# One reduction for the maxima of 16 scores, another layout of the scores, another buffer for the blocks' diagonal

## The chip, the cores and the metric

The kernel runs on one core of a Trainium2 chip. The core has a matrix engine (TensorE, PE in the profile), a vector engine (VectorE, DVE), a scalar engine (ScalarE, ACT), GpSimd (POOL) and SyncE (SP), whose queue here issues all transfers. Each takes its own instructions in the order in which they were written, and waits on semaphores for the others. The metric is the time on the device of one execution, in microseconds; several runs are made and the median is given.

## The reference

Two layers are computed, each made of the same two sublayers on 2048 tokens of 512 values. The first is a Fourier mixing, the second a product-key mixture of experts:

```python
def _A_ref(x, dft_seq_re, dft_seq_im, dft_hid_re, dft_hid_im):
    a = jnp.einsum("bsd,ed->bse", x, dft_hid_re)
    b = jnp.einsum("bsd,ed->bse", x, dft_hid_im)
    y = jnp.einsum("ts,bse->bte", dft_seq_re, a) - jnp.einsum("ts,bse->bte", dft_seq_im, b)
    return y

def _B_ref(x, w_q, k1, k2, u, v):
    ...
    s1 = jnp.einsum("nhd,ed->nhe", q1, k1)
    s2 = jnp.einsum("nhd,ed->nhe", q2, k2)
    i1 = jnp.argsort(-s1, axis=-1)[..., :K]
    i2 = jnp.argsort(-s2, axis=-1)[..., :K]
    t1 = jnp.take_along_axis(s1, i1, axis=-1)
    t2 = jnp.take_along_axis(s2, i2, axis=-1)
    cand = (t1[..., :, None] + t2[..., None, :]).reshape(BS, H, K * K)
    eidx = (i1[..., :, None] * E + i2[..., None, :]).reshape(BS, H, K * K)
    ord2 = jnp.argsort(-cand, axis=-1)[..., :K]
    top_s = jnp.take_along_axis(cand, ord2, axis=-1)
    top_e = jnp.take_along_axis(eidx, ord2, axis=-1)
    g = _softmax(top_s, axis=-1)
    ue = u[top_e]
    ve = v[top_e]
    act = _gelu(jnp.einsum("nd,nhkd->nhk", xf, ue))
    out = jnp.einsum("nhk,nhk,nhkd->nd", g, act, ve)

x = x + _A_ref(_layernorm(x, axis=-1), ...)
x = x + _B_ref(_layernorm(x, axis=-1), ...)
```

H is 32 heads, E 16 values in each of two halves (the two key sets), K is 2. So for every token, head and half the two largest of 16 scores are wanted with their places; of the four pairs the two best experts; and the 256 experts' activations are weighted by what all heads chose.

## The kernel before, in words

**Stages.** The hidden DFT is applied after the one along the sequence. `seq_unit` (line 434) multiplies the normalised tokens by a 256-token wide block of the sequence matrices (L518): 16 steps of 128 tokens, four accumulators, three matmuls for each, since all 32-bit numbers are split in a high and a low part. The blocks come from memory, and ACT and DVE split them (L458, L462). The result goes to `pth` and `ptl` (L543, L546). Seven units are 256 tokens wide; the last 256 tokens are two units of 128. `token_tile` (line 566) does everything else for 128 tokens: the hidden DFT (L615), the sum into the row (L625), the layer norm (L245 to L271), its transpose (L664 to L674), the scores (L694, L698) and the experts' inner products (L725), the search of the two largest, the weights, the output (L1044, L1048) and the sum into the row (L1064). There are 32 token tiles, 16 in each layer.

**Order.** Nothing is scheduled by hand. Each step is an `Op` with an engine, a duration by formula (`dve` at line 153, `act` at 157; a hop between dependent instructions of 0.13 us for DVE, line 76), what it follows, which buffers it takes and gives back, and a priority. `Plan.run` (line 89) plays the list through with these durations and draws the order on every engine from it. A pool in `BUFS` (line 176) gives the number of buffers; a `Hold` is one buffer taken from the first to the last user. PE's steps of token tiles get `late` 1.0 us in most of the program (line 121): the planner counts their inputs as so much later. The priority `FINAL` is that of the very last token tile, called `fine` in the code. Where PE has a gap behind the last sequence step, matmuls whose result nobody reads are put in (L1137).

**The search.** `f_sc` (L700) has ACT copy the scores of a half from PSUM (there as head, value) into `t["sc"]`, kept as value, half, head. `chain` (L773) then works on 16 x 64 scores. `tree32` (L781) takes the largest by four maxima of pairs, of 8, 4, 2 and 1 times 64 values; the partial results lie in `tmp`, the last goes to `val`. `eq` (L776) compares all scores with it, `codes` (L815) turns hits into place numbers, `tree16` (L795) reduces them to the place, `f_one` and `f_off` (L825, L829) push the found score far down, and the same is done again for the second. `flat` and `four` (L752, L755) are views of the scores and of `eq`. For the last token tile (`HALVED`) the two halves are separate chains of half the width. The small instructions from L854 to L892 choose the pairs and their weights; `q` is transposed (L903) and copied to `qt` (L907).

**The masks and the blocks.** For each half `hf` of the heads' groups, two masks `t["m", hf, r]` are made from `qt` (L926), the second is multiplied by the weights (L932), and PE multiplies them (L943). They take one `"lr"` buffer each, of four. The blocks' diagonal is copied by ACT (`f_gs`, L955) to `t["gs"]`, which takes a buffer of the pool `"sc"`, the one in which the scores lie; that pool has one buffer. From there SP sends it to memory and back in another order (L999, L1006), and DVE multiplies the activations by it (`f_weigh`, L1014). In the last token tile of a wide unit before the end (`spare_p`), and in the last of all, `gs` lies in the place of `pth` instead; the last token tile uses other buffers for its masks too, and no memory.

Of the kernel before, what the change touches and what calls it, by code (L numbers as in the profile page):

```python
# [8 lines left out]
F32 = mybir.dt.float32  # L9
# [7 lines left out]
P = 128  # L17
# [10 lines left out]
H = 32  # L28
# [124 lines left out]
def dve(n, rate=1):  # L153
    return 0.069 + n / (0.96e3 * rate)
# [11 lines left out]
def spectral_peer_kernel(ctx: ExitStack, tc, x_in, cseq, ctile, dhid, wq, k1t, k2t, ut, vm, out):  # L166
# [7 lines left out]


    BUFS = {"acc": 4, "bank": 4, "raw": 4, "c": 3, "p": 1, "row": 4, "wr": 5, "wp": 2,
            "tok": 3, "sc": 1, "eq": 1, "act": 3, "q": 2, "top": 1, "qt": 1, "lr": 4, "gt": 1, "pp": 1, "gdr": 2, "bn": 1}
    plan = Plan(BUFS)


# [47 lines left out]
    def work(shape, dtype, name, pool=None):  # L228
        return work_pool().tile(shape, dtype, name=name, bufs=BUFS[pool or name])
# [336 lines left out]
    def token_tile(layer, n, i, t0, at):  # L566
# [119 lines left out]
        for hf in range(2):  # L686
            hb = Hold("bank")

            def f_pch(hf=hf, ks=ks[0]):
                if ks.start == 0:  # L690
                    t["pc", hf] = bank([P, H, E])
                for k in range(ks.start, ks.stop):
                    for r in (wh, wl):
                        nc.tensor.matmul(t["pc", hf], t["th"][:, k, :], r[:, k, hf], start=(k == 0 and r is wh), stop=False)  # L694

            def f_pcl(hf=hf):
                for k in range(KD):
                    nc.tensor.matmul(t["pc", hf], t["tl"][:, k, :], wh[:, k, hf], start=False, stop=(k == KD - 1))  # L698

            def f_sc(hf=hf):  # L700
                if hf == 0:
                    t["sc"] = work([P, E, 2, H], F32, "sc")
                nc.scalar.copy(t["sc"][:, :, hf, :], t["pc", hf].rearrange("p h e -> p e h"))  # L703
# [12 lines left out]
            sc_parts.append(op("ACT", act(512), f_sc, [a_pe] + sc_parts, take=[hsc] if hf == 0 else [], last=[hb], prio=prio))  # L716
# [35 lines left out]
        def four(name):  # L752
            return t[name].rearrange("p e (f h) -> p e f h", f=2)

        def flat(name):  # L755
            return t[name].rearrange("p e f h -> p e (f h)")


        halved = HALVED(layer, at)
# [5 lines left out]
        def new():  # L765
            if "val" not in t:
                t["val"] = work([P, 2, 64], F32, "val", "top")
                t["tmp"] = work([P, E // 2, 64], F32, "tmp", "eq")
                t["eq"] = work([P, E, 64], F16, "eq")
                t["q"] = work([P, 3, 2, 2, H], F16, "q")  # L770
                t["key"] = work([P, 2, H], F16, "key", "top")

        def chain(z, fs, cols, w, after, prio):  # L773
            nf = fs.stop - fs.start

            def eq(rank_):  # L776
                def f():
                    nc.vector.tensor_tensor(t["eq"][:, :, cols], flat("sc")[:, :, cols], val(rank_, cols), op=ALU.is_equal)  # L778
                return f

            def tree32(rank_, after):  # L781
                def f0():
                    new()
                    nc.vector.tensor_max(t["tmp"][:, :, cols], flat("sc")[:, :8, cols], flat("sc")[:, 8:, cols])  # L784

                a = [op("DVE", dve(8 * w), f0, after, take=[heq, hq, htop] if rank_ == 0 and z == 0 else [], prio=prio)]
                for m in (4, 2, 1):
                    def f(m=m):
                        s = t["tmp"][:, :, cols]
                        o = s[:, :m] if m > 1 else t["val"][:, rank_, cols][:, None, :]  # L790
                        nc.vector.tensor_max(o, s[:, :m], s[:, m:2 * m])
                    a = [op("DVE", dve(w * m), f, a, prio=prio)]
                return a

            def tree16(dst, after):  # L795
                a = after
                for m in (8, 4, 2):
                    def f(m=m):
                        s = t["eq"][:, :, cols]
                        nc.vector.tensor_max(s[:, :m], s[:, :m], s[:, m:2 * m])  # L800
                    a = [op("DVE", dve(w * m, 2), f, a, prio=prio)]

                def f():
                    x, y = (t["eq"][:, m, cols].rearrange("p (f h) -> p f h", h=H) for m in (0, 1))
                    dst(x, y)
                return [op("DVE", 0.12, f, a, prio=prio)]

            def key1(x, y):
                x, y = (m[:, :, None, :].to_broadcast([P, nf, 2, H]) for m in (x, y))
                nc.vector.tensor_max(t["q"][:, fs, 0], x, y)  # L810

            def key2(x, y):
                nc.vector.tensor_max(t["key"][:, fs], x, y)

            def codes(after):  # L815
                def f():
                    e = four("eq")[:, :, fs]
# [3 lines left out]
            a = tree32(0, after)  # L821
            a = codes([op("DVE", dve(16 * w), eq(0), a, prio=prio)])
            a = tree16(key1, a)

            def f_one():  # L825
                k = t["q"][:, fs, 0, 0, :][:, None, :, :].to_broadcast([P, E, nf, H])
                nc.vector.tensor_tensor(four("eq")[:, :, fs], io[:, :, fs], k, op=ALU.is_equal)

            def f_off():  # L829
                s = flat("sc")[:, :, cols]  # L830
                nc.vector.scalar_tensor_tensor(s, t["eq"][:, :, cols], -BIG, s, op0=ALU.mult, op1=ALU.add)

            a = op("DVE", dve(16 * w, 2), f_one, a, prio=prio)
            a = op("DVE", dve(16 * w), f_off, [a], prio=prio)
            a_val = tree32(1, [a])
# [79 lines left out]
            return m[:, :, None, :].to_broadcast([P, 16, E, 4])  # L915


        made, hls = [], []

        soon = (0, 1, -1, i) if layer and at == len(units) - 2 else prio  # L920
        for hf in range(2):
            for r in range(2):
                def f_m(hf=hf, r=r):
                    io2 = iota[:, :, 0:4][:, None, :, :].to_broadcast([P, 16, E, 4])
                    t["m", hf, r] = piece((16, E, 4), ("ch", "cl")[r], F16) if fine else work([P, 16, E, 4], F16, "lr")
                    nc.vector.tensor_tensor(t["m", hf, r], io2, row_of(r, hf), op=ALU.is_equal)  # L926

                hls.append(Hold("lr") if not fine else hls[-1] if r else Hold("c"))
                a = op("DVE", dve(1024, 2), f_m, [a_qt], take=[] if fine and r else hls[-1:], prio=soon)

            def f_w(hf=hf):
                nc.vector.tensor_mul(t["m", hf, 1], t["m", hf, 1], row_of(2, hf))  # L932

            made.append(op("DVE", dve(1024, 2), f_w, [a], last=[hqt] if hf else [], prio=FINAL + soon[3:] if hf and soon != prio else soon))
        spare_p = fine or soon != prio and i == tiles_of(n)[-1]
        hgs, hbs = Hold("p" if spare_p else "sc"), [Hold("bank") for _ in range(2)]

        def f_blocks(hfs=(0, 1)):
            for hf in hfs:
# [10 lines left out]
        def f_gs(hf):  # L950
            def f():
                if hf == 0:
                    t["gs"] = work([P, 16, 4, E], F32, "sc") if not spare_p else mixed().rearrange(
                        "p (g t e) -> p g t e", t=4, e=E)
                nc.scalar.activation(t["gs"][:, 8 * hf:8 * hf + 8], t["pg", hf].rearrange("p g e t -> p g t e"),  # L955
                                     AF.Copy, scale=0.5 / GSCALE)
            return f
# [233 lines left out]
```

## Time and profile before

| what | value |
| --- | --- |
| median of 3 runs | 1266.33 us (1266.11 to 1267.36) |
| the profiled execution's own time | 1266.79 us |
| its span, first to last instruction | 1264.9 us |
| granted clock of TensorE | 1.00 |
| PE, share of the chain that ended last | 71% |
| DVE, share of that chain | 16% |
| mean rate of the transfers | 96 GB/s |

The span is the time between the first and the last instruction that the profiler recorded; the execution's own time has what lies around it. A busy share is an average over stages that have different limits. Matmuls are pipelined: the shown durations overlap, and the pace is the distance between their starts. In the chain of work, the time of a piece is what it added to the path, without what it shared with the piece before. The first 185 us prepare the weights; from there to about 1222 us token tiles and units of the sequence run beside each other; after it only the last token tiles are left.

### The profile page before, as it was taken

How to read it: one execution, taken by the hardware profiler on the slowest of the kernel's cores; microseconds unless marked ns; L12 is line 12 of the kernel's file. 1: busy time of each engine (PE TensorE's matmuls, PEld its weight loads, DVE VectorE, ACT ScalarE, POOL GpSimd, SP SyncE). 2: the span in 40 equal slices, each digit the busy share in tenths (PEclk: the TensorE clock that was granted, in tenths of full speed). 3: DMA queues.
4: the chain of work that ended last, by engine and by line, in shares of the span. 5: the costliest groups of instructions: out<-in, count | busy, mean ns of one | idle time of the engine just before them, and what ended most of it. 6: DMA issues, size and time to landing. Idle time of an engine off the chain costs nothing.

```text
span 1264.9 us, 20684 instructions
## 1 busy us (share of the span) xinstructions
PE 1250.8 (99%) x7804; PEld 1036.8 (82%) x7804; DVE 994.2 (79%) x2257; ACT 466.5 (37%) x966; POOL 45.7 (4%) x71
## 2 busy tenths in 40 slices
PE   9999999999999999999999999999999999999998
PEld 6777778887888888899878887888888888888886
DVE  8899998988887957779884378695685847778598
ACT  7522243343433333333563333333332433333232
POOL 2010000000000000000000000000000000000000
PEclk9999999999999999999999999999999999999999
DMA  7866541333233241413455204314142331414201
GB/s 235 268 197 213 180 150 34 92 70 65 67 84 76 76 101 50 112 39 88 121 133 135 67 26 104 81 59 109 42 108 51 93 91 51 108 43 110 58 9 35
DMA packets 224101, 121.18 MB, mean 96 GB/s; under 512 B 136448, under 2 KB 202496, under 8 KB 224000
## 3 DMA queue, kind: packets, MB, share of 16 engines
q1 hardware_dynamic: 224000, 119.85, 35.4%
q8 instruction: 61, 1.00, 0.3%
q14 instruction: 40, 0.33, 0.1%
HBM read 107.36 MB, written 12.45 MB: 95 GB/s over the span
## 4 chain that ended last, share of the span: by engine, by line
PE 71%; DVE 16%; issue 6%; DMA 2%; ACT 2%; SPq 1%; POOL 1%; POOLq 0%; DVEq 0%; ACTq 0%
PE acc L518 39%; PE bank L615 11%; PE bank L694 7%; PE bank L698 4%; PE bank L725 3%; DVE cl L462 2%; DVE w L384 2%; PE bank L1044 2%; DVE w L381 2%; PE bank L518 1%; PE bank L943 1%; DVE eq L778 1%; PE bank L1048 1%; PE bank L664 1%; POOL stats L260 1%
## 5 line engine op out<-in xcount | busy, mean ns | idle before, releaser
L518 PE MATMUL acc<-ch,xh 128*128 128x512 f32 (+1 forms) x1072 | 407.9, 381 | 0.0
L518 PE MATMUL acc<-ch,xl 128*128 128x512 f32 (+1 forms) x1072 | 397.8, 371 | 0.3 <-DVE xl L287 0.3
L518 PE MATMUL acc<-cl,xh 128*128 128x512 f32 (+1 forms) x1072 | 397.8, 371 | 0.0
L458 ACT CAST ch<-raw 128x512 fp32r<-128x512 f32 x256 | 158.4, 619 | 263.7 <-PE acc L518 227.0
L462 DVE TENSOR_TENSOR cl<-raw,ch 128x512 fp32r<-128x512 f32 x256 | 175.5, 687 | 72.4 <-ACT ch L458 52.9
L518 PEld LDWEIGHTS acc<-cl,xh 128*128 128x128 f32 x1072 | 201.9, 188 | 35.2
L518 PEld LDWEIGHTS acc<-ch,xh 128*128 128x128 f32 x1072 | 202.1, 189 | 32.6 <-issue 1.4
L518 PEld LDWEIGHTS acc<-ch,xl 128*128 128x128 f32 x1072 | 202.5, 189 | 31.6 <-DVE xl L287 1.0
L615 PE MATMUL bank<-dh,pth 128*128 128x512 f32 (+1 forms) x264 | 102.9, 392 | 0.4 <-ACT pth L543 0.4
L694 PE MATMUL bank<-wh,tok 128*128 128x512 f32 x256 | 100.2, 392 | 1.3 <-ACT sc L955 1.0
L615 PE MATMUL bank<-dl,pth 128*128 128x512 f32 (+1 forms) x264 | 100.6, 383 | 0.0
L694 PE MATMUL bank<-wl,tok 128*128 128x512 f32 x256 | 99.7, 390 | 0.0
L615 PE MATMUL bank<-dh,ptl 128*128 128x512 f32 (+1 forms) x264 | 95.9, 384 | 0.0
L784 DVE TENSOR_TENSOR tmp<-sc 128x512 f32<-128x512 f32 (+1 forms) x66 | 44.4, 672 | 61.7 <-ACT sc L703 60.8
L926 DVE TENSOR_TENSOR lr<-iota,qt 128x1024 f16<-128x1024 f16 x124 | 80.6, 684 | 10.6 <-ACT qt L907 10.6
L260 POOL TENSOR_TENSOR stats<-stats,half 128x1 f32<-128x1 f32 x64 | 44.4, 697 | 1183.7 <-DVE stats L257 1182.5
L778 DVE TENSOR_TENSOR eq<-sc,val 128x1024 f16<-128x1024 f32 (+1 forms) x66 | 78.5, 1190 | 1.5
L703 ACT COPY sc<-bank 128x512 f32<-128x512 f32 x64 | 36.8, 589 | 104.1 <-PE bank L698 73.1
L698 PE MATMUL bank<-wh,tok 128*128 128x512 f32 x256 | 68.5, 389 | 0.0
L800 DVE TENSOR_TENSOR eq<-eq 128x256 f16<-128x256 f16 (+3 forms) x198 | 60.0, 303 | 1.6
L615 PEld LDWEIGHTS bank<-dh,pth 128*128 128x128 f32 x264 | 49.6, 188 | 10.4 <-ACT pth L543 0.9
L694 PEld LDWEIGHTS bank<-wh,tok 128*128 128x128 f32 x256 | 48.1, 188 | 11.6 <-ACT raw L271 1.1
(152 smaller groups left out, 1790.7 us busy)
## 6 DMA issues: line engine op xcount, KB each, us to landing
raw<-in_cseq SPq DMA_DIRECT2D x224, 256.0 KB, 2.8
wr<-in_wq SPq DMA_DIRECT2D x32, 512.0 KB, 4.1
raw<-in_ctile SPq DMA_DIRECT2D x32, 256.0 KB, 2.9
wr<-in_x SPq DMA_DIRECT2D x16, 256.0 KB, 3.4
row<-in_x SPq DMA_DIRECT2D x16, 256.0 KB, 3.1
x2d<-row SPq DMA_DIRECT2D x16, 256.0 KB, 2.0
row<-x2d SPq DMA_DIRECT2D x16, 256.0 KB, 3.2
out<-row SPq DMA_DIRECT2D x16, 256.0 KB, 2.3
```

The source lines that it names most:

```text
L260: nc.gpsimd.tensor_tensor(st[:, 1:2], st[:, 1:2], half, op=ALU.pow)
L458: nc.scalar.copy(t[1], t[0])
L462: nc.vector.tensor_sub(t[2], t[0], as32(t[1]))
L518: nc.tensor.matmul(target(d), w[:, s, d * P:(d + 1) * P], moving(s % per, part), start=(s == 0 and k == 0 and d % blocks == 0), stop=(s == ...
L615: nc.tensor.matmul(t["y", cs.start], w[:, k, c, t0:t0 + P], r[:, c, k, cs], start=(z == 0 and c == 0 and m == 0), stop=(z == len(steps) - ...
L694: nc.tensor.matmul(t["pc", hf], t["th"][:, k, :], r[:, k, hf], start=(k == 0 and r is wh), stop=False)
L698: nc.tensor.matmul(t["pc", hf], t["tl"][:, k, :], wh[:, k, hf], start=False, stop=(k == KD - 1))
L725: nc.tensor.matmul(t["xu"], w[:, k, :], r[:, k, :], start=(m == 0), stop=(m == 3 * KD - 1))
L778: nc.vector.tensor_tensor(t["eq"][:, :, cols], flat("sc")[:, :, cols], val(rank_, cols), op=ALU.is_equal)
L784: nc.vector.tensor_max(t["tmp"][:, :, cols], flat("sc")[:, :8, cols], flat("sc")[:, 8:, cols])
L800: nc.vector.tensor_max(s[:, :m], s[:, :m], s[:, m:2 * m])
L926: nc.vector.tensor_tensor(t["m", hf, r], io2, row_of(r, hf), op=ALU.is_equal)
```

## The change

The scores are kept as half, head, value. The maximum of 16 is one `tensor_reduce` over the innermost axis, and `tmp` goes. `flat` becomes a transposed view, so that `eq` and `f_off` read the scores at a step of 16 values, 64 bytes, while `eq`'s own result keeps its layout. The masks of both halves of the groups lie in one buffer each for `r` = 0 and 1, so `"lr"` has two buffers of twice the size. The diagonal is copied into the buffer of the first masks (`t["mm", 0]`, read as 32-bit values), which is then held until the transfers have read it, and no longer takes the scores' buffer. The last token tile's masks and the places in `pth` stay as they were.

```diff
-            "tok": 3, "sc": 1, "eq": 1, "act": 3, "q": 2, "top": 1, "qt": 1, "lr": 4, "gt": 1, "pp": 1, "gdr": 2, "bn": 1}
+            "tok": 3, "sc": 1, "eq": 1, "act": 3, "q": 2, "top": 1, "qt": 1, "lr": 2, "gt": 1, "pp": 1, "gdr": 2, "bn": 1}
...
-                    t["sc"] = work([P, E, 2, H], F32, "sc")
-                nc.scalar.copy(t["sc"][:, :, hf, :], t["pc", hf].rearrange("p h e -> p e h"))
+                    t["sc"] = work([P, 2, H, E], F32, "sc")
+                nc.scalar.copy(t["sc"][:, hf], t["pc", hf])
...
-        def flat(name):
-            return t[name].rearrange("p e f h -> p e (f h)")
+        def flat():
+            return t["sc"].rearrange("p f h e -> p e (f h)")
...
-                t["tmp"] = work([P, E // 2, 64], F32, "tmp", "eq")
...
-                    nc.vector.tensor_tensor(t["eq"][:, :, cols], flat("sc")[:, :, cols], val(rank_, cols), op=ALU.is_equal)
+                    nc.vector.tensor_tensor(t["eq"][:, :, cols], flat()[:, :, cols], val(rank_, cols), op=ALU.is_equal)
...
-            def tree32(rank_, after):
-                def f0():
+            def largest(rank_, after):
+                def f():
                     new()
-                    nc.vector.tensor_max(t["tmp"][:, :, cols], flat("sc")[:, :8, cols], flat("sc")[:, 8:, cols])
...
+                    nc.vector.tensor_reduce(t["val"][:, rank_, cols], t["sc"].rearrange("p f h e -> p (f h) e")[:, cols],
+                                            axis=AX.X, op=ALU.max)
+
+                return [op("DVE", dve(16 * w), f, after, take=[heq, hq, htop] if rank_ == 0 and z == 0 else [], prio=prio)]
...
-                s = flat("sc")[:, :, cols]
+                s = flat()[:, :, cols]
                 nc.vector.scalar_tensor_tensor(s, t["eq"][:, :, cols], -BIG, s, op0=ALU.mult, op1=ALU.add)
...
-        made, hls = [], []
+        made, first_m, hls = [], [], [Hold("lr") for _ in range(2)] if not fine else []
+        spare_p = fine or layer and at == len(units) - 2 and i == tiles_of(n)[-1]
...
-                    t["m", hf, r] = piece((16, E, 4), ("ch", "cl")[r], F16) if fine else work([P, 16, E, 4], F16, "lr")
+                    if fine:
+                        t["m", hf, r] = piece((16, E, 4), ("ch", "cl")[r], F16)
+                    else:
+                        if hf == 0:
+                            t["mm", r] = work([P, 2, 16, E, 4], F16, "lr")
+                        t["m", hf, r] = t["mm", r][:, hf]
...
-                a = op("DVE", dve(1024, 2), f_m, [a_qt], take=[] if fine and r else hls[-1:], prio=soon)
+                if fine:
+                    hls.append(hls[-1] if r else Hold("c"))
+                a = op("DVE", dve(1024, 2), f_m, [a_qt], take=([] if r else hls[-1:]) if fine else [] if hf else [hls[r]],
+                       behind=first_m[r:r + 1] if hf else [], prio=soon)
+                first_m.append(a)
...
-        hgs, hbs = Hold("p" if spare_p else "sc"), [Hold("bank") for _ in range(2)]
+        hgs, hbs = Hold("p") if spare_p else hls[0], [Hold("bank") for _ in range(2)]
...
-                    t["gs"] = work([P, 16, 4, E], F32, "sc") if not spare_p else mixed().rearrange(
-                        "p (g t e) -> p g t e", t=4, e=E)
+                    m = mixed() if spare_p else t["mm", 0].rearrange("p f g e t -> p (f g e t)").bitcast(F32)
+                    t["gs"] = m.rearrange("p (g t e) -> p g t e", t=4, e=E)
...
-                           [pe[hf]] + evac, take=[] if hf else [hgs], last=hbs[hf:hf + 1], prio=prio))
+                           [pe[hf]] + evac, take=[hgs] if spare_p and not hf else [], last=hbs[hf:hf + 1], prio=prio))
```

More of the change, by code (lines that the diff above doesn't have):

```diff
@@ L777, in f @@
                 def f():
-                    nc.vector.tensor_tensor(t["eq"][:, :, cols], flat("sc")[:, :, cols], val(rank_, cols), op=ALU.is_equal)
+                    nc.vector.tensor_tensor(t["eq"][:, :, cols], flat()[:, :, cols], val(rank_, cols), op=ALU.is_equal)
                 return f
-            def tree32(rank_, after):
-                def f0():
+            def largest(rank_, after):
+                def f():
                     new()
[L784 to L793, printed above, removed]
+                    nc.vector.tensor_reduce(t["val"][:, rank_, cols], t["sc"].rearrange("p f h e -> p (f h) e")[:, cols],
+                                            axis=AX.X, op=ALU.max)
+                return [op("DVE", dve(16 * w), f, after, take=[heq, hq, htop] if rank_ == 0 and z == 0 else [], prio=prio)]
             def tree16(dst, after):
@@ L819, in codes @@
                 return [op("DVE", dve(16 * w, 2), f, after, prio=prio)]
-            a = tree32(0, after)
+            a = largest(0, after)
             a = codes([op("DVE", dve(16 * w), eq(0), a, prio=prio)])
@@ L834, in chain @@
             a = op("DVE", dve(16 * w), f_off, [a], prio=prio)
-            a_val = tree32(1, [a])
+            a_val = largest(1, [a])
             a = op("DVE", dve(16 * w), eq(1), a_val, last=[hsc], prio=prio)
@@ L924, in f_m @@
                     io2 = iota[:, :, 0:4][:, None, :, :].to_broadcast([P, 16, E, 4])
-                    t["m", hf, r] = piece((16, E, 4), ("ch", "cl")[r], F16) if fine else work([P, 16, E, 4], F16, "lr")
-                    nc.vector.tensor_tensor(t["m", hf, r], io2, row_of(r, hf), op=ALU.is_equal)
-                hls.append(Hold("lr") if not fine else hls[-1] if r else Hold("c"))
-                a = op("DVE", dve(1024, 2), f_m, [a_qt], take=[] if fine and r else hls[-1:], prio=soon)
+                    if fine:
[4 more added lines that the diff above has]
+                        t["m", hf, r] = t["mm", r][:, hf]
+                    nc.vector.tensor_tensor(t["m", hf, r], io2, row_of(r, hf), op=ALU.is_equal)
+                if fine:
[3 more added lines that the diff above has]
+                first_m.append(a)
             def f_w(hf=hf):
@@ L934, in token_tile @@
             made.append(op("DVE", dve(1024, 2), f_w, [a], last=[hqt] if hf else [], prio=FINAL + soon[3:] if hf and soon != prio else soon))
-        spare_p = fine or soon != prio and i == tiles_of(n)[-1]
-        hgs, hbs = Hold("p" if spare_p else "sc"), [Hold("bank") for _ in range(2)]
+        hgs, hbs = Hold("p") if spare_p else hls[0], [Hold("bank") for _ in range(2)]
         def f_blocks(hfs=(0, 1)):
```

## The prediction

> **What bounds the kernel now.** I read the page first, then the stages by windows, then the order of the instructions.
>
> ```profile
> span 1264.9 us, 20684 instructions
> ...
> PE 1250.8 (99%) x7804; PEld 1036.8 (82%) x7804; DVE 994.2 (79%) x2257; ACT 466.5 (37%) x966; POOL 45.7 (4%) x71
> ```
>
> PE is busy all the time, but the page warns that a busy PE need not be at its peak, so the pace of the matmuls has to be seen. From the timeline of PE in the second layer:
>
> ```profile
> 1000.09 0.39 PE L518 MATMUL acc<-ch,xl 128*128 128x512 f32 x1
> ...
> 1000.77 0.39 PE L518 MATMUL acc<-ch,xl 128*128 128x512 f32 x1
> ```
>
> These two are three matmuls apart: 0.68 us for three, 0.227 us each, while each is shown as 0.39 us. They overlap, and PE takes the next one at an even pace. What the change can give back there is only what PE waits for. In the view of waits, PE's own (us in total, times, longest), those that hang on the stage of the change are:
>
> ```profile
> PE bank L1023 <- DVE act L1014: 2.0, 4, 0.8
> PE bank L694 <- ACT sc L955: 1.0, 1, 1.0
> ...
> PE bank L903 <- DVE q L870: 0.5, 2, 0.3
> ```
>
> Together 3.5 us in the whole span. The middle is PE's, and 3.5 us bounds a gain there. The end is not. The windows (length, then PE, PEld, DVE, ACT, POOL busy) and one group of instructions:
>
> ```profile
> 640.00:1200.00 560.00, 558.78 (x3119) 464.59 (x3118) 391.07 (x891) 199.02 (x411) 11.41 (x18) 1.00 0.32 81
> ...
> 1235.66:1249.26 13.60, 13.42 (x94) 10.97 (x92) 13.20 (x57) 2.87 (x8) 0.00 (x0) 1.00 0.19 21
> 1249.26:1264.90 15.64, 11.40 (x130) 7.58 (x130) 9.82 (x19) 3.12 (x8) 0.00 (x0) 0.98 0.14 51
> ...
> L1137 PE MATMUL acc<-dh 128*128 128x512 f32 x58 | 14.5, 396 | 0.0
> ```
>
> L1137 is the filler that keeps PE occupied when there is nothing to multiply. So PE's 13.42 us of 13.60 is no work: from 1235.66 to 1249.26 the last tile's top-2 search runs on DVE, 13.20 us busy of 13.60, and everything waits for it. **DVE bounds these 13.6 us, PE the 1220 before.**
>
> **The maxima.** From the groups by line and form (last numbers: busy us, mean ns of one):
>
> ```profile
> L778 DVE TENSOR_TENSOR eq<-sc,val 128x1024 f16<-128x1024 f32 x62 | 75.8, 1222 | 1.5
> ...
> L784 DVE TENSOR_TENSOR tmp<-sc 128x512 f32<-128x512 f32 x62 | 42.7, 689 | 61.6 <-ACT sc L703 60.8
> ...
> L791 DVE TENSOR_TENSOR tmp<-tmp 128x256 f32<-128x256 f32 x62 | 26.2, 422 | 1.3
> ...
> L791 DVE TENSOR_TENSOR tmp<-tmp 128x128 f32<-128x128 f32 x66 | 19.1, 289 | 1.6
> ...
> L397 DVE TENSOR_REDUCE ws<-bank 128x128 f32<-128x384 f32 x32 | 18.0, 561 | 0.0
> ...
> L791 DVE TENSOR_TENSOR val<-tmp 128x64 f32<-128x64 f32 x62 | 13.8, 223 | 1.6
> ```
>
> A maximum now is 689 + 422 + 289 + 223 = 1623 ns in four dependent instructions. The new one reads 1024 elements once. The only reductions of size are L397's: 561 ns for 384 elements, where the rows at 256 and 512 elements (422, 689) give 556 in between, so a reduction lies on the same line as the others, and at 1024 elements that line has 1222 (L778). Bounds: 561 / 384 x 1024 = 1.50 us above; below, 1.07 us, the slope (1222 - 689) / 512 with no fixed part. I take 1.22: 0.40 us saved, twice on each of 31 tiles, 24.9 us of DVE. Up to 1200 us it lies beside PE's matmuls and is worth nothing but a part of the 3.5 us; I take 0.5, with 0 and 3.5 as ends.
>
> [...]
>
> **In the last tile** the search is cut in two halves, so the reduction has 512 elements. From DVE's and ACT's timeline, and behind them the chain of work:
>
> ```profile
> 1234.83 0.59 ACT L703 COPY sc<-bank 128x512 f32<-128x512 f32 x1 [2.85 <-PE bank L698]
> 1235.66 0.42 DVE L784 TENSOR_TENSOR tmp<-sc 128x256 f32<-128x256 f32 x1
> 1236.11 0.55 DVE L791 TENSOR_TENSOR tmp<-tmp 128x128 f32<-128x128 f32 x2
> 1236.69 0.19 DVE L791 TENSOR_TENSOR val<-tmp 128x32 f32<-128x32 f32 x1
> 1236.92 0.69 DVE L778 TENSOR_TENSOR eq<-sc,val 128x512 f16<-128x512 f32 x1
> ```
>
> ```profile
> 1244.73 0.34 DVE tmp L784
> ...
> 1245.26 0.20 DVE tmp L791
> ...
> 1245.60 0.13 DVE tmp L791
> ...
> 1245.84 0.12 DVE val L791
> ...
> 1246.29 0.60 DVE eq L778
> ```
>
> The first maximum runs alone: 1236.92 - 1235.66 = 1.26 us, against 0.69 and about 0.03 to the next, 0.54 saved. The other three run between instructions of the other half, which hide their latency, so they cost only what the chain shows: 0.34 + 0.20 + 0.13 + 0.12 = 0.79, against 0.60 for 512 elements, 0.19 saved each. Sum 0.54 + 3 x 0.19 = 1.1 us. With fewer instructions to lay between them the halves may show up to 0.3 us more latency; the start (scores copied at 1235.42, DVE there at 1235.66) may come up to 0.2 earlier, because the tile before it gets 0.8 us shorter. I leave these two against each other: **1.1 us**. What is late next is the way behind 1249.26 us, masks, blocks and store.
>
> **Strided reads.** Scores now lie with the value innermost, so L778, twice a tile, and L831, once, read them (L831 also writes) with a step of 16 values, 64 bytes. No instruction of DVE here reads SBUF at that step. Nearest are L210, a reduction of SBUF at a step of 16 bytes (L209 the same data unstrided), and L1012, which reads PSUM at 64 bytes:
>
> ```profile
> 1.49 0.48 DVE L209 TENSOR_REDUCE picks<-identf 128x32 f32<-128x128 f32 x1
> 1.69 0.37 DVE L210 TENSOR_REDUCE picks<-identf 128x4 f32<-128x128 f32 x1
> 1.92 0.06 DVE L206 MEMSET half<- 128x1 f32 x1
> ...
> L1012 DVE TENSOR_TENSOR act<-act,bank x1: 420/420/420, 1258.3 to 1258.3; 128x256 f32<-128x256 f32 x1
> ```
>
> L210 gives way to the next after 0.23 us, L209 after 0.20, for 128 elements; a read at half pace would have added 128 x 1.04 = 0.13, not 0.03. L1012's 420 ns are L791's 422 at 256 elements. Both speak for no cost; I take 0. Upper end: half pace, 1.07 us for each of the three. [...] The copy L703 writes the same 512 values; I take no change.
>
> [...]
>
> **The diagonal's buffer.** The copy L955 used to take the one score buffer, so it stood behind the next tile's last read of its scores:
>
> ```profile
> ACT sc L955 <- DVE eq L778: 38.3, 15, 6.1
> ...
> gdr<-sc SPq DMA_DIRECT2D x120, 32.0 KB, 2.1
> ...
> 926.49 0.70 PE L943 MATMUL bank<-lr 128*64 128x64 f16 x32
> ...
> 939.02 0.69 DVE L926 TENSOR_TENSOR lr<-iota,qt 128x1024 f16<-128x1024 f16 x1 [0.25 <-ACT qt L907]
> ```
>
> It now follows its own blocks, and the next tile's scores no longer wait for its DMAs. The 38.3 us are idle ACT; PE felt 1.0 of them, which is in the 3.5 above. The new wait: the next tile's first masks stand on DVE behind the landing of the diagonal, and behind them in that queue whatever DVE does next, with PE's blocks after it. Blocks to next masks are 12.5 us at the tightest pair; blocks 0.7, two copies of 0.6, four issues in 2.6 us and 2.1 us of landing make 6.6. It is covered, with 6 us to spare. Near the end it brings something. Tile 12's blocks and copy stand so on PE and ACT, and the last row, of the chain, is the weighting that came of it:
>
> ```profile
> 1215.87 0.69 PE L943 MATMUL bank<-lr 128*64 128x64 f16 x32
> ...
> 1225.06 1.09 ACT L955 ACTIVATE sc<-bank 128x512 f32<-128x512 f32 x2 [2.19 <-DVE eq L778]
> ...
> 1250.89 0.34 DVE pl L1031
> ```
>
> The copy can come 8 us earlier, and then this L1031 need not stand among the last tile's masks: 0.34 us on the path, and perhaps more from the row sum before L742. I take 0.4, ends 0 and 0.9.
>
> **Sum.** 1.1 + 0.4 + 0.5 = 2.0 us. The profiled execution took 1266.79 us, 1.9 around its span, 0.46 above the median, so it stands for the median: 1266.33 - 2.0 = **1264.3 us**.
>
> **Rivals.** 1. *More comes back* (0.30, faster): all of 3.5, 0.9 and 1.1 is 5.5 us, 1260.8; with half of the waits, 3.75 us, 1262.6. For it: the waits are those of this stage. Against: they come from the list order, which is drawn anew, so new ones arise.
> 2. *The strided reads cost* (0.15, slower): at half pace a tile's search grows by 3 x 1.07 = 3.2 us. The planner (lines 76 and 153) counts the maximum 0.53 us shorter, four instructions with three hops of 0.13 against one, the rows 0.40, so the search is 3.2 + 2 x 0.13 = 3.5 us later than planned. How much is covered shows here, where DVE is done at 1008.12 and PE transposes at 1009.39:
>
> ```profile
> 1007.90 0.22 DVE L892 TENSOR_TENSOR q<-gw,q 128x64 f16<-128x64 f32 x1
> ...
> 1009.39 0.28 PE L903 MATMUL bank<-ident,q 128*128 128x128 f16 x2
> ```
>
> 1.27 us. PE would wait 2.2 us in each of 31 tiles, 68 us, and the end would lose 3.2 - 1.1: up to 1336 us. It decides from 0.34 us an operation on; below that only the end feels it.
> 3. *A new wait in the list order* (0.05, slower): one or two stalls of some us where masks or DMAs come later than planned, about 1271 us.
> 4. *Nothing arrives* (0.08, same): the halves show the latency that the tree hid, 1266.3 us.
>
> **How the numbers follow.** My forecast has 0.42, from 1263.8 to 1266. A measurement can tell about 0.2%, 2.5 us, from no change: below 1263.8 is faster, above 1268.9 slower. Forecast and rival 4 are the same: 0.50; rival 1 faster: 0.30; rivals 2 and 3 slower: 0.20. The range goes from 1261.5 to 1275 us; the upper part of rival 2 and the end of rival 1 are left out.
>
> **What would show it.** Right: reductions of 1.2 us (0.69 in halves); L778's and L831's successors still at 1222 ns; DVE from the last tile's first maximum to its L870 about 12.5 us, not 13.6; even PE at 0.227 us. Wrong: L778 at 1.5 us or more, waits of L903 on DVE in every tile, L926 waiting for the diagonal's DMA, or a stretch behind the last search that is longer than 15.6 us.

## The result, and the profile after

The changed kernel is slower: 1319.66 us, median of 4 runs (1318.15 to 1321.84), against 1266.22 us for the kernel before on the same chip. The ratio is 1.0421, 95% interval 1.0402 to 1.0441. The profiled execution took 1321.84 us. Its page, with the lines that answer to those shown of before:

```profile
span 1320.1 us, 20463 instructions
...
PE 1265.4 (96%) x7801; PEld 1041.0 (79%) x7801; DVE 1040.2 (79%) x2059; ACT 463.3 (35%) x966; POOL 49.2 (4%) x71
...
PE 44%; DVE 41%; issue 9%; ACT 3%; DMA 2%; POOL 1%; SPq 0%; DVEq 0%; POOLq 0%; ACTq 0%
```

The span grew by 55.2 us. PE's idle time (span less busy) went from 14.1 to 54.7 us, the rest is PE showing longer busy for the same matmuls. DVE has 198 instructions fewer and is busy 46 us more. The last line is the chain that ended last, by engine: DVE's share rose from 16% to 41%. The groups by line and form, DVE alone (busy us, mean ns of one), the first line from the kernel before, the others from the changed one:

```profile
L831 DVE SCALAR_TENSOR_TENSOR sc<-eq,sc 128x1024 f32<-128x1024 f16 x31 | 37.9, 1223 | 0.8
```

```profile
L777 DVE TENSOR_TENSOR eq<-sc,val 128x1024 f16<-128x1024 f32 x62 | 120.2, 1938 | 0.9
...
L783 DVE TENSOR_REDUCE val<-sc 128x64 f32<-128x1024 f32 x62 | 75.4, 1217 | 70.8 <-ACT sc L703 69.9
L824 DVE SCALAR_TENSOR_TENSOR sc<-eq,sc 128x1024 f32<-128x1024 f16 x31 | 63.3, 2042 | 0.7
...
L777 DVE TENSOR_TENSOR eq<-sc,val 128x512 f16<-128x512 f32 x4 | 4.2, 1041 | 0.0
```

The reduction (L783) takes 1217 ns, as forecast. The comparison (L777) went from 1222 to 1938 ns and the push-down (L824, L831 before) from 1223 to 2042. Between 512 and 1024 elements the comparison's slope is (1938 - 1041) / 512 = 1.75 ns an element, 1.68 times the (1222 - 689) / 512 = 1.04 before. That makes 2 x 0.72 + 0.82 = 2.25 us more a tile, and with the 0.26 us by which the planner now counts the two maxima shorter than they are, each search ends **2.5 us later than planned**, measured against the kernel before. What PE does then, in its waits and in the timeline of one tile's end, DVE first:

```profile
PE bank L896 <- DVE q L863: 20.3, 22, 3.0
PE bank L896 <- DVE q L885: 9.0, 13, 0.9
```

```profile
1196.94 2.06 DVE L824 SCALAR_TENSOR_TENSOR sc<-eq,sc 128x1024 f32<-128x1024 f16 x1
1199.04 1.22 DVE L783 TENSOR_REDUCE val<-sc 128x64 f32<-128x1024 f32 x1
1200.29 1.95 DVE L777 TENSOR_TENSOR eq<-sc,val 128x1024 f16<-128x1024 f32 x1
...
1205.91 0.22 DVE L863 TENSOR_TENSOR q<-key,df 128x128 f16<-128x128 f16 x1
```

```profile
1206.20 0.28 PE L896 MATMUL bank<-ident,q 128*128 128x128 f16 x2 [0.64 <-DVE q L863]
1207.40 0.23 PE L896 MATMUL bank<-ident,q 128*128 128x128 f16 x1 [0.92 <-DVE q L885]
1207.44 0.47 PE L518 MATMUL acc<-ch,xh 128*128 128x512 f32 x1
```

The transposes of `q` (L896, before L903) stand in PE's list ahead of sequence matmuls that have their data; PE takes its list in order, so L518 waits with them. These waits were 0.5 us in the span before and are 29.3 now. In the second layer's window (length, then PE, PEld, DVE busy) they are nearly all of PE's idle time:

```profile
640.00:1200.00 560.00, 542.13 (x3004) 445.97 (x3003) 400.64 (x784) 196.54 (x408) 11.13 (x17) 1.00 0.31 80
```

PE is idle 17.9 us of 560, against 1.2 before, and the two rows' waits inside that window add up to 16.5.

### The profile page after: what moved, and what is told of

Read it like the earlier page. It is cut to its first block, busy times and chain, and to the rows that moved or that the text cites. A ratio compares the mean times of both kernels' runs of the same rounds, so it can differ in the third digit from the quotient of the medians.

```text
span 1320.1 us, 20463 instructions
## 1 busy us (share of the span) xinstructions
PE 1265.4 (96%) x7801; PEld 1041.0 (79%) x7801; DVE 1040.2 (79%) x2059; ACT 463.3 (35%) x966; POOL 49.2 (4%) x71
## 4 chain that ended last, share of the span: by engine, by line
PE 44%; DVE 41%; issue 9%; ACT 3%; DMA 2%; POOL 1%; SPq 0%; DVEq 0%; POOLq 0%; ACTq 0%
PE acc L518 20%; PE bank L615 9%; DVE eq L777 6%; DVE cl L462 6%; DVE sc L824 4%; PE bank L694 4%; DVE val L783 4%; DVE eq L793 3%; DVE lr L925 2%; DVE w L384 2%; DVE eq L811 2%; PE bank L698 2%; PE bank L518 2%; PE bank L1046 2%; DVE w L381 2%
## 5 line engine op out<-in xcount | busy, mean ns | idle before, releaser
L518 PE MATMUL acc<-ch,xh 128*128 128x512 f32 (+1 forms) x1072 | 409.6, 382 | 0.0
L518 PE MATMUL acc<-cl,xh 128*128 128x512 f32 (+1 forms) x1072 | 399.5, 373 | 1.1 <-DVE cl L462 1.1
L518 PE MATMUL acc<-ch,xl 128*128 128x512 f32 (+1 forms) x1072 | 399.4, 373 | 0.0
L518 PEld LDWEIGHTS acc<-cl,xh 128*128 128x128 f32 x1072 | 203.3, 190 | 37.9 <-DVE cl L462 2.0
L518 PEld LDWEIGHTS acc<-ch,xh 128*128 128x128 f32 x1072 | 203.6, 190 | 32.5 <-issue 0.8
L518 PEld LDWEIGHTS acc<-ch,xl 128*128 128x128 f32 x1072 | 203.8, 190 | 31.5 <-DVE xl L287 0.5
L783 DVE TENSOR_REDUCE val<-sc 128x64 f32<-128x1024 f32 (+1 forms) x66 | 78.2, 1185 | 71.1 <-ACT sc L703 70.2
L777 DVE TENSOR_TENSOR eq<-sc,val 128x1024 f16<-128x1024 f32 (+1 forms) x66 | 124.3, 1884 | 0.9
L694 PE MATMUL bank<-wh,tok 128*128 128x512 f32 x256 | 100.3, 392 | 0.6 <-ACT sc L703 0.6
L694 PE MATMUL bank<-wl,tok 128*128 128x512 f32 x256 | 99.8, 390 | 0.0
L260 POOL TENSOR_TENSOR stats<-stats,half 128x1 f32<-128x1 f32 x64 | 47.9, 752 | 1234.1 <-DVE stats L257 1232.9
L546 DVE TENSOR_TENSOR ptl<-acc,pth 128x512 fp32r<-128x512 f32 x62 | 42.2, 684 | 49.4 <-ACT pth L543 49.4
L824 DVE SCALAR_TENSOR_TENSOR sc<-eq,sc 128x1024 f32<-128x1024 f16 (+1 forms) x33 | 65.5, 1984 | 0.7
```

The lines of the kernel that those rows point to most:

```text
L260: nc.gpsimd.tensor_tensor(st[:, 1:2], st[:, 1:2], half, op=ALU.pow)
L518: nc.tensor.matmul(target(d), w[:, s, d * P:(d + 1) * P], moving(s % per, part), start=(s == 0 and k == 0 and d % blocks == 0), stop=(s == ...
L777: nc.vector.tensor_tensor(t["eq"][:, :, cols], flat()[:, :, cols], val(rank_, cols), op=ALU.is_equal)
L783: nc.vector.tensor_reduce(t["val"][:, rank_, cols], t["sc"].rearrange("p f h e -> p (f h) e")[:, cols], axis=AX.X, op=ALU.max)
```

## The experiments

The last sequence matmul splits each span into the middle and the end. By line L518's own view (count, shortest, median and longest ns, first and last start) it starts so, in the kernel before and then in the changed one:

```profile
L518 PE MATMUL acc<-cl,xh x1072: 278/389/402, 18.2 to 1222.0; 128*128 128x512 f32 x146, 128*128 128x256 f32 x33
```

```profile
L518 PE MATMUL acc<-cl,xh x1072: 278/389/628, 18.2 to 1274.3; 128*128 128x512 f32 x146, 128*128 128x256 f32 x33
```

It starts 52.3 us later. For all runs (times in us; "end" is from there to the end of the span; the two right columns come from one profiled execution of each kernel):

| run | median | ratio [95%] | last L518 against before | end |
| --- | --- | --- | --- | --- |
| before | 1264.4 to 1266.3 | 1 | 0 | 42.9 |
| the change | 1319.66 | 1.0421 [1.0402, 1.0441] | +52.3 | 45.8 |
| e1 reduction strided | 1293.71 | 1.0230 [1.0212, 1.0249] | +25.8 | 44.5 |
| e2 buffers alone | 1273.09 | 1.0059 [1.0044, 1.0074] | -4.9 | 54.7 |
| e3 layout alone | 1333.43 | 1.0538 [1.0522, 1.0554] | +59.0 | 48.6 |
| e4 planner told | 1282.92 | 1.0138 [1.0121, 1.0155] | +4.7 | 56.0 |
| e5 buffers, order mended | 1262.71 | 0.9983 [0.9974, 0.9992] | -1.8 | 43.1 |
| e6 step of 8 bytes | 1262.96 | 0.9980 [0.9971, 0.9989] | -3.0 | 43.1 |
| e7 step of 16 bytes | 1318.82 | 1.0423 [1.0407, 1.0439] | +47.8 | 47.4 |
| e8 2.44 us late | 1344.22 | 1.0629 [1.0605, 1.0653] | +70.3 | 48.3 |
| e9 1.22 us late | 1293.20 | 1.0220 [1.0205, 1.0235] | +24.1 | 46.5 |
| e10 told, transposes first | 1282.99 | 1.0141 [1.0124, 1.0158] | +4.9 | 56.2 |
| e11 told, masks first too | 1273.30 | 1.0067 [1.0051, 1.0084] | +1.8 | 46.0 |

**e1 to e4: the parts, and what the planner knows.** In e1 the scores lie as before, so that the comparison and the push-down read them side by side and the reduction reads them at 256 bytes.

```diff
-                    t["sc"] = work([P, 2, H, E], F32, "sc")
-                nc.scalar.copy(t["sc"][:, hf], t["pc", hf])
+                    t["sc"] = work([P, E, 2, H], F32, "sc")
+                nc.scalar.copy(t["sc"][:, :, hf, :], t["pc", hf].rearrange("p h e -> p e h"))
...
-            return t["sc"].rearrange("p f h e -> p e (f h)")
+            return t["sc"].rearrange("p e f h -> p e (f h)")
```

> The scores lie as before the change (value, half, head), so the comparisons (L778 before) and the push-down (L831 before) read without a step again; the reduction reads them at a step of 64 values, 256 bytes; the new buffers stay. Theory S (strided reads of SBUF on DVE cost, 1.75 ns an element instead of 1.04, and the time is lost because the search comes later than planned): comparisons back at 1222 ns, push-down at 1223, the reduction at about 1940 ns instead of 1217, so the search is 2 x 0.32 = 0.6 us longer than with the four maxima and about 1.7 us later than planned against before; that is 0.4 us over the 1.27 us of cover, some 13 us in all: about 1280 us. Rival B (the new buffers or the new list order cost the time): about 1319 us, comparisons at 1222 ns all the same. Rival N (the step costs only where there are two inputs): reduction at 1217 ns and about 1265 us.

```profile
L783 DVE TENSOR_REDUCE val<-sc 128x64 f32<-128x1024 f32 x62 | 123.5, 1991 | 71.1 <-ACT sc L703 70.3
...
L777 DVE TENSOR_TENSOR eq<-sc,val 128x1024 f16<-128x1024 f32 x62 | 75.6, 1219 | 0.9
```

The cost moved with the stride: the comparison is back at 1219 ns, the reduction at 1991. The time came out 14 us higher than expected of it, 1293.71.

e2 keeps the old layout and the tree of maxima, and has only the new buffers; e3 has the old buffers, and of the change only layout and reduction. The lines below show where e3 differs from the changed kernel in its buffers:

```diff
-            "tok": 3, "sc": 1, "eq": 1, "act": 3, "q": 2, "top": 1, "qt": 1, "lr": 2, "gt": 1, "pp": 1, "gdr": 2, "bn": 1}
+            "tok": 3, "sc": 1, "eq": 1, "act": 3, "q": 2, "top": 1, "qt": 1, "lr": 4, "gt": 1, "pp": 1, "gdr": 2, "bn": 1}
...
-        hgs, hbs = Hold("p") if spare_p else hls[0], [Hold("bank") for _ in range(2)]
+        hgs, hbs = Hold("p" if spare_p else "sc"), [Hold("bank") for _ in range(2)]
```

> Only the buffers of the change: masks of both halves in one buffer, the diagonal in the first one; maxima by four instructions, scores in the old layout. Theory S: the strided reads are gone, so 1266 us, 3 us either way for the new list order. Rival B: well above 1266, up to 1319 us, with L926 waiting for the diagonal's transfers.

> Only the layout and the reduction of the change; four mask buffers and the diagonal in the scores' buffer as before. Theory S: comparisons at 1940 ns, push-down at 2040 ns and about 1319 us, within 8 us. Rival B: comparisons just as slow, but the time near 1266 us, below 1280.

e3 says that layout and reduction carry the whole loss. Its 1333.43 us lie 14 us above the changed kernel and above what was expected, so the new buffers took some 14 us off the loss in the full change. e2 alone missed what was expected of it: its middle is 4.9 us shorter, its end 11.8 us longer. From e2's timelines, PE and then DVE:

```profile
1233.91 0.28 PE L725 MATMUL bank<-uh,tok 128*128 128x256 f32 x1
1234.03 0.34 PE L903 MATMUL bank<-ident,q 128*128 128x128 f16 x3
```

```profile
1226.64 0.22 DVE L870 TENSOR_TENSOR q<-key,df 128x128 f16<-128x128 f16 x1
...
1244.20 0.22 DVE L870 TENSOR_TENSOR q<-key,df 128x128 f16<-128x128 f16 x1
1244.34 1.28 DVE L932 TENSOR_TENSOR lr<-iota,qt 128x1024 f16<-128x1024 f16 x2
...
1264.32 0.42 DVE L1023 TENSOR_TENSOR act<-act,raw 128x256 f32<-128x256 f32 x1 [4.43 <-DMA raw<-gdr]
```

The next-to-last tile's `q` was ready at 1226.86, but its transposes stood behind the last tile's scores and inner products (L694 to L725) until 1234.03. Its masks (L932 on `lr`, from 1244.34) then fell behind the last tile's search on DVE, which ends with the second L870, and its diagonal came last of all. That is an accident of the list, and e5 mends it.

e4 is the changed kernel with the same instructions; only the durations that the planner counts with for the strided ones are set near what was measured.

```diff
-            a = codes([op("DVE", dve(16 * w), eq(0), a, prio=prio)])
+            a = codes([op("DVE", dve(16 * w, 0.57), eq(0), a, prio=prio)])
...
-            a = op("DVE", dve(16 * w), f_off, [a], prio=prio)
+            a = op("DVE", dve(16 * w, 0.54), f_off, [a], prio=prio)
...
-            a = op("DVE", dve(16 * w), eq(1), a_val, last=[hsc], prio=prio)
+            a = op("DVE", dve(16 * w, 0.57), eq(1), a_val, last=[hsc], prio=prio)
```

> The changed kernel with the planner told what the strided instructions take (1.94 and 2.04 us for a whole tile instead of 1.14 each), nothing else. Theory S, by way of lateness: DVE is as busy as in the changed kernel (1040 us), but PE's transposes stand 2.5 us a tile later in the list, so PE's waits for the search go from 29 us to under 8, and the time to about 1275 us, the rest being the longer search in the last tile (some 3 us) and the first token tiles, where DVE is nearly full. Rival W (it is the work itself that DVE cannot do in time): waits move elsewhere and the time stays above 1305 us.

The middle's loss fell from 52.3 to 4.7 us, and the waits for `q` went from PE's list; the largest there now is another (`PE acc L518 <- DVE xl L287`, 5.4 us, once). The strided instructions still take as long:

```profile
L777 DVE TENSOR_TENSOR eq<-sc,val 128x1024 f16<-128x1024 f32 x62 | 120.8, 1948 | 0.9
...
L824 DVE SCALAR_TENSOR_TENSOR sc<-eq,sc 128x1024 f32<-128x1024 f16 x31 | 63.3, 2041 | 0.7
```

So nearly all of the 52 us were lost because the order was drawn without the strides' time. What is left is 4.7 us against the kernel before, and 9.6 against e2, which has the same buffers and no stride. The wait of 5.4 us stands at 660 us, where the layers change; between 600 and 740 us the kernel before has none over 1.0 us, and e2, in its whole span, none over 0.9 us but the 2.0 us for `ident`. Whether the longer search itself or its new place in the list makes that wait was not tried. The time, 1282.92, missed the 1275 expected because the end grew to 56.0 us; e10 and e11 take that up.

**e5 to e7: from which step on it costs.** e5 is e2 with the next-to-last tile's transposes ahead.

```diff
-        a = op("PE", 3 * TR16 + 0.06, f_pq, [c5, d2], take=[hb], last=[hq], prio=prio)
+        ahead = layer and at == len(units) - 2 and i == tiles_of(n)[-1]
+        a = op("PE", 3 * TR16 + 0.06, f_pq, [c5, d2], take=[hb], last=[hq], prio=(0, 1, -3, i) if ahead else prio)
```

> The buffers of the change alone (as in the run before, 1273), with one priority altered: the transposes of the next-to-last tile's choices stand ahead of the last tile's scores in PE's list. Theory O (the buffers made the long stretch 4.9 us shorter, and all of it and more was lost because these transposes fell behind the scores, so that this tile's diagonal came back from memory last): the last sequence matmul stays at about 1217 us, the transposes come at about 1227 instead of 1234, nothing waits 4.4 us for the diagonal at the end, and the time is about 1261 us. Rival C (the end got longer for another reason, such as the transfers or the shared mask buffers): above 1268 us.

e6 and e7 are e5 with the reduction, the scores kept as (16 / b values, half, head, b values) with b = 2 in e6 and 4 in e7. The comparison's innermost step is then 8 or 16 bytes, and the push-down is cut in b instructions. For e6 the author guessed at 1222 ns in the comparison and about 1260 us, for e7 at about 1940 ns, as at 64 bytes, and 1280 us or more.

```diff
-                    t["sc"] = work([P, E, 2, H], F32, "sc")
+                    t["sc"] = work([P, E // 2, 2, H, 2], F32, "sc")
...
+                    nc.vector.tensor_reduce(t["val"][:, rank_, cols], t["sc"].rearrange("p a f h b -> p (f h) a b")[:, cols],
+                                            axis=AX.XY, op=ALU.max)
...
+                for b in range(2):
+                    s, e = flat(cols)[:, :, b], apart(t["eq"][:, :, cols])[:, :, b]
+                    nc.vector.scalar_tensor_tensor(s, e, -BIG, s, op0=ALU.mult, op1=ALU.add)
```

> One reduction for the maxima, but the scores in pairs: (pair, half, head, 2), so the comparisons read at a step of 2 values, 8 bytes, and the reduction reads pairs that are 512 bytes apart; the push-down is two instructions of half the size; buffers and order as in the first kernel of this call. [...] Rival M (any step costs): comparisons at about 1940 ns and 1285 us or more.

> [...] Rival F (up to four 32-bit values a step is free, which L210's 0.23 us at 16 bytes suggested): comparisons at 1222 ns and about 1261 us.

The groups by line and form of e6, and behind them of e7:

```profile
L781 DVE TENSOR_TENSOR eq<-sc,val 128x1024 f16<-128x1024 f32 x62 | 75.7, 1221 | 0.7
L787 DVE TENSOR_REDUCE val<-sc 128x64 f32<-128x1024 f32 x62 | 75.5, 1218 | 79.5 <-ACT sc L703 78.7
...
L829 DVE SCALAR_TENSOR_TENSOR sc<-eq,sc 128x512 f32<-128x512 f16 x62 | 40.1, 689 | 0.6
```

```profile
L781 DVE TENSOR_TENSOR eq<-sc,val 128x1024 f16<-128x1024 f32 x62 | 123.4, 1990 | 0.7
...
L787 DVE TENSOR_REDUCE val<-sc 128x64 f32<-128x1024 f32 x62 | 75.5, 1218 | 64.6 <-ACT sc L703 63.7
L829 DVE SCALAR_TENSOR_TENSOR sc<-eq,sc 128x256 f32<-128x256 f16 x124 | 68.8, 625 | 0.5
```

A step of 8 bytes costs nothing (1221 ns), one of 16 bytes costs nearly the same as 64 (1990 against 1938), and the time follows: 1262.96 against 1318.82. The push-down agrees: its halves at 8 bytes take 689 ns, as 512 values side by side do, and its quarters at 16 bytes 625 ns, where 256 values side by side take 422 (L791 before). The theory that a step of 16 bytes is free, on which the forecast stood, fell here.

e5 and e6 are each faster than the kernel before by 0.2%; they don't differ from one another. e6 has 21.6 us of DVE less in all (971.2 busy, against 992.8 in e5). Its last sequence matmul starts 1.2 us earlier, inside the 0 to 3.5 us that were forecast, and nothing of it is left in the time.

**e8 and e9: lateness alone.** The kernel before, with the first comparison written three times (e8) or twice (e9) over itself: contiguous work of 2.44 or 1.22 us a tile that the planner doesn't know of.

```diff
-                    nc.vector.tensor_tensor(t["eq"][:, :, cols], flat("sc")[:, :, cols], val(rank_, cols), op=ALU.is_equal)
+                    for _ in range(1 if rank_ else 3):
+                        nc.vector.tensor_tensor(t["eq"][:, :, cols], flat("sc")[:, :, cols], val(rank_, cols), op=ALU.is_equal)
```

> The kernel before, with its first comparison of each tile done three times over instead of once and the planner not told: 2.44 us more DVE work a tile, no strided read, old buffers. The changed kernel's search is 2.5 us later than planned. Theory S by way of lateness: PE waits for the search at L903 in nearly every tile, and the time is 50 to 65 us over the kernel before, 1315 to 1330. Rival D (strided reads also disturb others, so that lateness alone costs far less): under 1290 us.

> The kernel before, with the first comparison done twice in place of three times (nothing else strided or moved), so each tile's search is 1.22 us later than planned, half of the run with three. Theory of a cover (as in rival 2 of the prediction): 1.27 us of slack hide it, PE's waits for the search stay below 2 us, and only the last tile loses some 1.2 us: 1266 to 1269 us. Theory of a drift (lateness is paid in proportion, as each late tile makes later steps late too): half of 78 us, 1300 to 1310 us.

PE's waits in e8, and behind them in e9 (us in total, times, longest):

```profile
PE bank L944 <- DVE lr L933: 19.5, 12, 2.4
PE bank L904 <- DVE q L871: 11.9, 11, 3.0
```

```profile
PE bank L944 <- DVE lr L933: 5.9, 8, 0.9
PE bank L904 <- DVE q L871: 3.5, 3, 1.5
PE bank L725 <- ACT sc L956: 2.8, 2, 1.9
```

Without any stride, 2.44 us of lateness cost 79 us (e8, more than expected). e9 decides between the two ways in which lateness is paid: a cover of 1.27 us would have hidden 1.22 us, and 28 us were lost. Its largest waits are for the masks (L944 waits for L933), where the prediction had looked at the transposes only. It isn't proportional either: the time is below the 1300 us of the other theory, and twice the lateness cost 2.8 times as much.

**e10 and e11: what is left when the planner knows.** Both are e4 with the order at the end mended, e10 as in e5, e11 with the tile's masks ahead as well:

```diff
-        soon = (0, 1, -1, i) if layer and at == len(units) - 2 else prio
+        soon = (0, 1, -3, i) if ahead else (0, 1, -1, i) if layer and at == len(units) - 2 else prio
```

> The changed kernel, with the planner told what the strided operations take, and with the transposes of the next-to-last tile ahead of the last tile's scores. Theory that lateness and the order at the end are all there is: the sequence ends within 6 us of the kernel before, the end loses 1.1 us by the longer search, and the time is 1269 to 1275 us. Theory that the strided operations cost time of their own beside PE as well: no better than 1280 us.

e10 missed: moving the transposes was not enough. Its DVE in the end, where 1240.92 begins and 1255.72 ends the last tile's search, and L935 and the two rows of L926 on `lr` belong to the tile before it:

```profile
1240.92 0.68 DVE L783 TENSOR_REDUCE val<-sc 128x32 f32<-128x512 f32 x1
...
1255.72 0.22 DVE L863 TENSOR_TENSOR q<-key,df 128x128 f16<-128x128 f16 x1
1255.87 0.68 DVE L935 TENSOR_TENSOR lr<-lr,qt 128x1024 f16<-128x1024 f16 x1
1256.47 0.68 DVE L926 TENSOR_TENSOR lr<-iota,qt 128x1024 f16<-128x1024 f16 x1
...
1262.03 0.68 DVE L926 TENSOR_TENSOR lr<-iota,qt 128x1024 f16<-128x1024 f16 x1
...
1275.13 0.43 DVE L1017 TENSOR_TENSOR act<-act,raw 128x256 f32<-128x256 f32 x1 [5.32 <-DMA raw<-gdr]
```

> The run before this with one thing more: the first masks of the next-to-last tile go ahead of the last tile's search, as its transposes did. In that run the sequence ended 4.9 us later than in the kernel before, but the end behind it took 56 us in place of 43, since four mask instructions of that tile stood on DVE behind the whole search of the last tile and its diagonal came last. Theory that this order is what is left: the end shrinks to 45 to 48 us, the time is 1270 to 1276 us. Theory that strided operations cost more than their own length: still 1280 us or more.

With the masks ahead too, that weighting (L1017) comes at 1254.43 in place of 1275.13, the end takes 46.0 us and the time is 1273.30, as expected. DVE is busy 1038.0 us there, as much as in the changed kernel (1040.2). The change lost 53.4 us; all but 8.9 came back without one instruction made shorter.

## Why the prediction was wrong

**The step that failed** is the one on strided reads: "Both speak for no cost; I take 0". Each of the three operations costs 0.72 to 0.82 us, between the 0 taken and the upper end given, 1.07. The two rows it rested on could not carry it. L1012 reads PSUM, and the runs show that DVE does not price a step there as in SBUF: 256 values at 64 bytes from PSUM took 420 ns, as the 422 of L791 without a step, while 512 values at 64 bytes from SBUF took 1041 (L777), against 689 without. (L397, from which the reduction was priced, also reads PSUM at 64 bytes, and it too lies on the line without a step.) L210 does read SBUF at 16 bytes, the step that costs in e7; but by e7's row the surplus is (1990 - 1222) / 1024 x 128 = 0.10 us for its 128 elements, in an instruction whose distance to the next was 0.2 us anyway. That the short form hid it is argued, not tried.

The step from which it costs lies above 8 bytes and not above 16: the comparison takes 1221 ns in e6 and 1990 in e7. The reduction of e6, which reads two neighbours and then jumps 512 bytes, takes 1218 ns, and the one that reads its 16 values side by side 1217, so the jump from pair to pair cost nothing there. What in the engine or the memory makes the step cost, no run shows.

**Rival 2** is what happened, at a chance of 0.15, with other sizes: 1.68 times the time for each further element and not twice (half pace was a guess that no run shows), 2.5 us late and not 3.5. Two of the prediction's signs of being wrong came with it: the comparison's 1938 ns, and 35 waits of PE for the search. Its sum, lateness less a cover of 1.27 us, would then be (2.5 - 1.27) x 31 = 38 us. Measured were 52. e9 shows the wrong term: the cover read at one tile's transposes is not the smallest. Where else the 28 us of e9 arise is shown only in part. The three rows above hold 12 of them; PE's idle time grew by 18.8 in all (span less busy, 32.9 against 14.1), and the rest is PE showing longer busy. So "it decides from 0.34 us an operation on" is too high; from where it does was not tried.

**The maxima**: right. 1217 ns against 1.22 us, and e6 shows that what they save on DVE in the middle is worth nothing that the time shows.

**The last tile**: right for the reduction alone. In e6 from the first maximum (1233.77) to the end of the last `q` (L868, 1246.51 + 0.22 us) it is 13.0 us, in e5 (1234.16 to 1247.84 + 0.22) 13.9: 0.9 saved, forecast 1.1. It gave nothing, since the first maximum stands 14.8 us behind the last L518 in e6 and 14.0 in e5. In the changed kernel the windows (length, then PE, PEld and DVE busy) show the search at 14.87 us and not 12.5, by the strides:

```profile
1289.39:1304.26 14.87, 12.50 (x90) 10.21 (x88) 14.56 (x44) 3.48 (x10) 0.00 (x0) 1.00 0.22 36
1304.26:1320.10 15.84, 11.15 (x131) 8.19 (x131) 8.57 (x16) 1.97 (x5) 0.00 (x0) 1.00 0.09 34
```

The stretch behind it is 15.84 us against 15.64: nothing new came up there.

**The diagonal's buffer**: the wait was covered as forecast. DVE nowhere sat idle before the masks for the diagonal's transfer, in e2 as in the change; only for the copy of `qt`, 1.4 us. The size was wrong in both directions. Put at 0.4 us, it is a loss of 8.3 us alone (e2), through the end's order, and a gain of 2.6 once that is mended (e5; the kernel before with the mended order alone was not run). The bound of 3.5 us on a gain in the middle was passed in e2 (4.9 us, in one profile), with the buffers alone. Rival 3, a new wait in the list order, is e2's end; it was priced at 5 us and came to 11.8. In the changed kernel itself it did not arise (end 45.8 us).

**The sum of 2.0 us** came near what e6 gives, which has the change without its strides and a mended order: 1262.96 against 1265.26 on the same chip, 2.3 us. That is luck. The sum had 1.1 us from the reduction in the last tile and 0.4 from the buffers; e5, which has no reduction, already gains 2.6, and the reduction adds nothing.

## What to carry to other kernels

Before a layout is turned, give each reader its step in bytes, and price a step that the trace doesn't show from a row of the same memory and of the same length, or count the full upper end. Where an order is drawn from assumed durations, an operation that runs over its assumed time can cost the bounding engine most of the excess, although its own engine has idle time: here 2.5 us in each of 31 tiles, 78 us in all, cost 52 us, and 4.7 once the order knew of them. After any edit that draws such an order anew, read the end of the chain separately, since one tile's steps that fall behind another's search cost 10 to 12 us there (e10 against e11, e2 against e5).

## What the runs showed of the hardware

A one-input reduction pays for the stride like a two-input comparison (1991 and 1938 ns for 1024 32-bit values), 16, 64 and 256 bytes pay nearly the same (1990, 1938, 1991), and 8 bytes pay nothing (1221, against 1222 side by side). All steps tried are powers of two.

Some time after a wait PE can run at about half its pace for a few microseconds. From the changed kernel's timeline of PE:

```profile
691.10 0.34 PE L896 MATMUL bank<-ident,q 128*128 128x128 f16 x3 [3.05 <-DVE q L863]
...
692.03 0.40 PE L518 MATMUL acc<-ch,xh 128*128 128x512 f32 x1
692.26 0.39 PE L518 MATMUL acc<-ch,xl 128*128 128x512 f32 x1
...
692.81 0.63 PE L518 MATMUL acc<-ch,xh 128*128 128x512 f32 x1
693.24 0.63 PE L518 MATMUL acc<-ch,xl 128*128 128x512 f32 x1
...
696.13 0.39 PE L518 MATMUL acc<-cl,xh 128*128 128x512 f32 x1
```

The distance between starts is 0.23 us right after the wait, 0.43 from 692.81 on, and 0.23 again from 696.13 on; the granted clock is 0.51 from 692.80 to 696.10 us, and 0.96 in the window from 680 to 720 us. The wait of 3.05 us so cost some 1.5 us more. The same kernel has two more such stretches: behind its wait of 2.45 us at 336.41 (clock 0.50 from 338.50 to 341.00), and behind that of 2.04 us at 1258.82, where matmuls of 256 columns start 0.21 us apart and from 1262.71 on 0.12 (clock 0.70 from 1260.50 to 1264.00). But behind its wait of 2.42 us at 1304.31 the clock is 1.00. So the runs give no length of a wait from which on it happens. In e8 the longest matmul of L518 takes 796 ns, at a granted clock of 0.990, in e9 504 ns, at 0.999. That may be a part of why twice the lateness cost more than twice: an estimate from the two clocks is (0.999 - 0.990) x 1340.6 = 12 us of e8's 79. Twice e9's 28 is 57, so some 10 us stay open.
